# Attention units on TensorE regrouped by array tiling, the next tile's mask among the whole-array products

## The chip, the cores and the metric

The program runs on one core of one Trainium2 chip. The metric is device time in microseconds of one launch. The kernel before took 776.3 us (median of 3 runs, 775.83 to 776.98).

## The reference, cut to what matters

The program is an attention block and two mixture-of-experts layers one after the other. The attention (4 batches, 8 heads, 576 positions, head width 64) adds two parts: a softmax over keys pooled by four, and a local softmax over the keys less than four positions away.

```python
q_d = q.reshape(B, H, Sd, factor, D).mean(axis=3)      # k_d, v_d alike
out_up = np.repeat(sm_attn(q_d, k_d, v_d), factor, axis=2)
mask = np.abs(pos[:, None] - pos[None, :]) < factor     # factor = 4
scores = np.where(mask, scale * q @ k.T, -1e9)
out_local = softmax(scores) @ v
x = (out_up + out_local) rearranged to 2304 tokens x 512
x = moe(x)         # top-1 of 8 experts, tokens with x @ w_skip > 0
return moe2(x)     # top-2 of 8 experts, with noise on the logits
```

## The kernel before, in words

The first 130 us or so hold the attention, the rest the two expert layers. Attention is cut into **units**: 18 local tiles of 128 tokens (class `Local`, all 8 heads, four quarters of 32 tokens with a window of 38 keys each) and 5 pooled units per batch (class `Pooled`). `push(unit)` writes out one step of a software pipeline. TensorE, ScalarE and VectorE execute what `push` records in exactly that order; SyncE's queue of DMAs is ordered by the scheduler.

A step holds, for the newest unit, `scores` (products into a bank `pA`; for a local tile first a mask product with the whole array, L952, then 16 products of 32 columns, L958) and `soft` (VectorE: row maximum and difference, L965/L967 or L845/L848). For the unit two steps back it holds `turn` (transposes into `pT`, L983 or L859, and a ScalarE copy). Then come the step's fill functions, and among them or behind them the new unit's `exp` on ScalarE (L977 or L853), which waits for VectorE's `soft`. Last come the `values` of the unit three steps back (L996 for a local tile, L873 for a pooled unit) and VectorE's division (L1001, L877/L884).

The fill functions finish a token tile: `x_add` (adds the pooled part, L1007), `x_turn` (four transposes L1013, ScalarE copy L1015 into `xT`), in the next step `x_part` (products with the gate weights in four column strips of 32, L1022, ScalarE copy L1025 into `xpart`), and one step later `x_logits` (L1031, then L1032 on VectorE and L1033 on ScalarE) and the store of the tile (L1040 on SyncE's queue). `pool_v` (L805, L812) pools the values of a batch.

TensorE is used in two tilings. Whole-array products are those with 128x128 behind the operation's name in the trace (transposes, mask, logits, pooled scores and values). Column-tiled products address a strip of 32 columns and show as 128*32: the scores and values of local tiles, `x_part`, the fifth pooled unit of each batch and `pool_v`.

Buffers that matter here: `pT` has 3 banks, `pA` 2, `pB` 2; the copies `xT` have `NXT = 2` buffers; the finished tiles `x` have `XB = 8`. When no unit is left, `push(None)` drains the pipeline, and the last tiles pass through turn, part and logits behind each other; then TensorE turns the tokens gathered for the first expert (L541, `pT<-ident,xr`) and goes on with that expert's products (L562).

Of the kernel before, what the change touches and what calls it, by code (L numbers as in the profile page):

```python
# [23 lines left out]
NT = N // 128  # L24
# [3 lines left out]
W = 38  # L28
# [77 lines left out]
def moe_attention_kernel(ctx, tc, q, k, v, w_skip, w_gate, w1, w2, g2, n2, noise, u1, u2, out, dbg=None):  # L106
    nc = tc.nc
# [21 lines left out]
    def bank(tag, shape, dtype=F32):  # L129
        return psums[0].tile(shape, dtype, name=tag, tag=tag, bufs=psum_bufs[tag])  # L130
# [16 lines left out]
    identb = consts.tile([128, 128], BF, name="identb")  # L147
# [213 lines left out]
    late = rt.tile([128, NT], F32, name="late")  # L361
# [257 lines left out]
    with ExitStack() as actx:  # L619
# [92 lines left out]
        def mask(d):  # L712
            if d not in masks:
                distances(d)
                m = masks[d] = at.tile([128, 8, W], BF, name="mask" + "".join(map(str, d)), bufs=1)
                nc.vector.tensor_tensor(scr, dj[d], dj[d], op=OP.mult)
                nc.vector.tensor_scalar(m, scr[:, None, :].to_broadcast([128, 8, W]), 9.5, -8e9, op0=OP.is_gt,
                                        op1=OP.mult)
            return masks[d]

        offsets = [tuple(window(4 * t + s)[3] for s in range(4)) for t in range(NT)]
# [99 lines left out]
        class Pooled:  # L821
# [8 lines left out]
            def scores(self):  # L830
                b, u = self.b, self.u
                kd = kds[b % 2]
                assert held["kd", b % 2] == (b, 10)
                p = bank("pA", [128, 2, NPOOL])
                if u < 4:
                    nc.tensor.matmul(p, qd[b][:, u, 0:128], kd[:, u], start=True, stop=True)
                else:
                    for i in range(4):
                        nc.tensor.matmul(p[32 * i:32 * i + 32], qd[b][:, i, 112:144], kd[:, i], start=True,
                                         stop=True, tile_position=(0, 32 * i), skip_group_check=True)  # L840
                self.p = p
# [83 lines left out]
        def expand_up(t):  # L925

            b = B - 1
            p = ups[t] = bank(UPT, [128, DM])
            c = 64 + 128 * t - S * b
            x = expand[0]  # L930
            if t < NT - 1:
                nc.tensor.matmul(p, x[:, c:c + 128], od[b], start=True, stop=t > NT - 5, skip_group_check=True)
            for i in range(4):
                r, ci = p[:, i * 128:(i + 1) * 128], 64 + i * 128
                if t == NT - 5:
                    nc.tensor.matmul(r[0:64], x[:, ci + 64:ci + 128], ors[b - 1], start=False, stop=True,
                                     skip_group_check=True)
                elif t == NT - 1:
                    nc.tensor.matmul(r, x[:, ci:ci + 128], ors[b], start=True, stop=True, skip_group_check=True)

        class Local:
# [3 lines left out]
            def __init__(self, t):  # L945
                self.tile_no = t

            def scores(self):
                t = self.tile_no
                win = [window(4 * t + s) for s in range(4)]  # L950
                p = bank("pA", [128, 8, W])
                nc.tensor.matmul(p, identb, mask(offsets[t]), start=True, stop=False,  # L952
                                 skip_group_check=True)
                for i in range(4):
                    for s in range(4):
                        b, s0, ks, _ = win[s]
                        assert held["k", b % 2] == b
                        nc.tensor.matmul(p[s * 32:s * 32 + 32, 2 * i:2 * i + 2, :], qT[b][:, i, s0:s0 + 32],  # L958
                                         kTs[b % 2][:, :, i, ks:ks + W], start=False, stop=True,
                                         tile_position=(0, 32 * s), skip_group_check=True)  # L960
                self.p = p

            def soft(self):
                mx = at.tile([128, 8], F32, name="mx", bufs=NES)
# [78 lines left out]
        pipe = []  # L1043
        later = {}

        def schedule(n, f, *args):
            later.setdefault(len(pipe) + n, []).append(lambda: f(*args))

        drain = []
        wide = ep.tile([128, KF * CAPS[0]], F32, name="wide", tag="hT1")  # L1050
# [42 lines left out]

        def finish(t):
            if t in UPE:
                later.setdefault(len(pipe), []).insert(0, lambda: expand_up(t))
            elif t < SWIFT:
                schedule(UP, load_up, t)
            add = 0 if t in UPE else 2 if t >= SWIFT else ADD
            schedule(add, x_add, t)  # L1100
            add += STAY.get(t, 0)
            schedule(add + TURN, x_turn, t)
            schedule(add + PART, x_part, t)
            schedule(add + LOGIT, x_logits, t)
            if t == TA - 1:
                schedule(ADD + LOGIT - 4 + TA0, start_routing)

        def push(unit, *fill):
            fill = list(fill) + later.pop(len(pipe), [])
            pipe.append(unit)  # L1110
            if unit:
                unit.scores()
                unit.soft()
            if len(pipe) > D1 and pipe[-1 - D1]:
                pipe[-1 - D1].turn()
            for i, f in enumerate(fill):
                if i == 2 and unit:
                    unit.exp()
                f()
            if len(fill) <= 2 and unit:  # L1120
                unit.exp()
            if unit:
                for i in range(FILL + FILLS.get(len(pipe), 0)):
                    nc.tensor.matmul(wp, warm[:, 0:128], warm, start=True, stop=True)
            un = pipe[-1 - D2] if len(pipe) > D2 else None
            if un:
                un.values()
                t = un.tile_no
                if t is None:
                    if un.u == 3:  # L1130
                        ready.add(un.b)
                        if un.b == B - 1:
                            for n in range(SWIFT, UPE[0]):
                                schedule(0, load_up, n)
                else:
                    waiting.append(t)
                    if t + NVW < NT:
                        load_local(t + NVW)
            if started:
                run(early_1 or (early_2 if len(pipe) > PA else []), RS[min(len(started), len(RS)) - 1])  # L1140
                started.append(True)
                if len(pipe) > LA:
                    run(early_load, 1)
                if len(pipe) > LB:
                    run(early_load_2, 1)
                if len(pipe) > GA:
                    run(early_gather)
                if len(pipe) > TURN1:
                    run(early_turn)
                run(early_up, UP1.get(len(pipe), 0))  # L1150
            for i in range(1 if unit else DRAIN):
                if waiting and batch_of(waiting[0]) in ready:
                    finish(waiting.pop(0))
# [36 lines left out]
        pooled_after = {}  # L1190
# [3 lines left out]
        for t in range(NT):  # L1194
            for b in range(B):
                if LOADQK[b] == t:
                    load_qk(b)
                    if b in ONPOOLQD:
                        schedule(QDP, pool_q, b)
                if POOLQK[b] == t:  # L1200
                    for n in range(8):
                        schedule(n // QKS, pool_qk, b, n)
                    for n in range(3):
                        schedule(n // 2 if b in ONDVE else n, pool_qk, b, n + 8)
                if b == 0 and t == EXP4 and UPE:
                    schedule(0, expansion)
                if POOLV[b] == t:
                    schedule(0, pool_v, b, 0)
                    schedule(VS, pool_v, b, 1)
            if t == 3:  # L1210
                load_wall()
            if t < 3:
                schedule(0, lambda: None)
                schedule(0, lambda: None)
                schedule(0, (start_1, start_2, start_3)[t])
            push(Local(t))
            for b, u in pooled_after.get(t, []):
                push(Pooled(b, u))
        drain.append(True)
        while later or waiting or any(pipe[-D2:]):  # L1220
            push(None)
# [410 lines left out]
    with ExitStack() as mctx:  # L1632
# [20 lines left out]
        with none1.Else():  # L1653
            run(over1.steps[8:] + spilled())
            with tc.For_i(0, n_over1, 1) as i:
# [13 lines left out]
                p = bank("pH", [BLK1, 5, 1])  # L1669
# [34 lines left out]
        for e in range(E):  # L1704
# [9 lines left out]
            for f2 in range(KF // 2):  # L1714
# [6 lines left out]
                if f2 == 2 and e == 0:  # L1721
                    p = bank("pT", [BLK1, 3, C1])
# [57 lines left out]
    whole = Whole(weight_slot(F32), weight_slot(F32))  # L1780
# [78 lines left out]
    for e in range(1, E):  # L1859
# [17 lines left out]
        for b in range(NB2):  # L1877
# [6 lines left out]
            i = e * NB2 + b  # L1884
# [4 lines left out]
    with tc.If(n_over2 > 0):  # L1889
        with tc.For_i(0, n_over2, 1) as i:  # L1890
# [17 lines left out]
            p = bank("pH", [BLK2, 5, 1])  # L1908
# [10 lines left out]
            p = bank("pT", [128, KD, BLK2])  # L1919
# [6 lines left out]
            for f in range(KF):  # L1926
                p = bank("pH", [128, BLK2])
# [3 lines left out]
            p = bank("pY", [BLK2, DM])  # L1931
# [49 lines left out]
```

## Time and profile before

| | |
|---|---|
| median of 3 runs | 776.3 us |
| the profiled execution | 775.65 us |
| its span | 773.8 us |
| TensorE busy | 751.3 us, 97% |
| VectorE busy | 354.1 us, 46% |
| ScalarE busy | 249.1 us, 32% |
| granted TensorE clock, mean | 0.996 |

The span is the time between the first and the last profiled instruction. Busy shares are averages over stages with different limits: over the whole span VectorE is busy 46% of the time, but between 80 and 100 us 16.90 us of 20. TensorE's ends are modelled, so that "busy" there means occupied; the distance from one start to the next shows what a group of products really takes.

### The profile page before, as it was taken

The page shows a single profiled execution, that of the slowest core. Times are in us where ns is not written, and L with a number is a line of the kernel's source. Part 1 is how long each engine was busy: PE and PEld are TensorE (multiplying, and loading weights), DVE is VectorE, ACT ScalarE, POOL GpSimd, SP SyncE. Part 2 cuts the span into 40 slices and gives each one's busy share as a digit, 9 for nine tenths or more (in the row PEclk, how much of TensorE's full clock was granted, in tenths as well). Part 3 has the DMA queues.
Part 4 walks back from the last instruction along what each step waited for, and adds up shares of the span by engine and source line. Part 5 has one row for each costly group of instructions (what it writes and reads, how often), then busy time and mean ns, then how long its engine had stood idle before and what let it go on. Part 6 is the DMA issues. An engine that isn't in the chain of part 4 may idle for free.

```text
span 773.8 us, 15147 instructions
## 1 busy us (share of the span) xinstructions
PE 751.3 (97%) x6216; PEld 663.1 (86%) x6217; DVE 354.1 (46%) x794; ACT 249.1 (32%) x492; POOL 253.2 (33%) x259
## 2 busy tenths in 40 slices
PE   6799999999999999999999999999999999999996
PEld 3476777999999999988998998998997997987984
DVE  8886887411111755559864342352343342342200
ACT  3354553111112143224334333233333232333211
POOL 8781522220232432033565115115115125002012
PEclk9999999999999999999999999999999999999999
DMA  8898559599988872341647626426336336323013
GB/s 289 276 303 280 148 162 338 162 368 352 336 312 269 298 249 72 102 79 53 169 140 187 180 73 170 111 91 171 88 110 159 78 119 157 94 82 58 8 17 46
DMA packets 60264, 130.73 MB, mean 169 GB/s; under 512 B 15489, under 2 KB 16320, under 8 KB 58656
## 3 DMA queue, kind: packets, MB, share of 16 engines
q1 hardware_dynamic: 30688, 55.85, 22.9%
q0 software_dynamic: 12256, 27.21, 16.8%
q10 hardware_dynamic: 17248, 46.66, 16.7%
q8 instruction: 50, 0.82, 0.4%
q14 instruction: 22, 0.18, 0.1%
HBM read 101.86 MB, written 23.91 MB: 163 GB/s over the span
## 4 chain that ended last, share of the span: by engine, by line
PE 77%; issue 2%; DVE 1%; DMA 1%; POOL 0%; ACT 0%; POOLq 0%; DVEq 0%; ACTq 0%
PE pY L1622 27%; PE pH L1605 26%; PE pH L562 9%; PE pY L577 9%; PE pT L1590 2%; PE pT L599 1%; DMA rows<-x_d,ix2g 1%; PE pT L541 1%; PE pT L348 1%; PE pH L588 0%; POOL out L319 0%; DVE w L339 0%; PE pH L604 0%; PE pT L225 0%; DVE hl L1610 0%
## 5 line engine op out<-in xcount | busy, mean ns | idle before, releaser
L1622 PE MATMUL pY<-w,hh 128*128 128x512 f32 (+6 forms) x640 | 201.4, 396 | 0.0
L1605 PE MATMUL pH<-xh,w 128*128 128x256 f32 (+7 forms) x1024 | 195.9, 303 | 0.0
L1605 PEld LDWEIGHTS pH<-xh,w 128*128 128x128 f32 x1024 | 162.8, 188 | 0.8
L1622 PEld LDWEIGHTS pY<-w,hh 128*128 128x128 f32 (+6 forms) x640 | 115.0, 183 | 27.6
L1281 DVE TENSOR_TENSOR w<-stg,w 128x1024 fp32r<-128x1024 f32 x64 | 82.7, 1300 | 109.2 <-ACT w L1280 109.1
L1622 PE MATMUL pY<-w,hl 128*128 128x512 f32 (+6 forms) x320 | 125.7, 393 | 0.0
L1605 PE MATMUL pH<-xl,w 128*128 128x256 f32 (+7 forms) x512 | 123.4, 302 | 0.0
L1610 DVE SCALAR_TENSOR_TENSOR hl<-pH,hh 128x256 fp32r<-128x256 f32 (+7 forms) x128 | 56.9, 473 | 127.6 <-ACT hh L1609 127.3
L319 POOL DMA_INDIRECT out<-yo,ix2w x35 | 68.6, 1960 | 130.2 <-ACT yo L1624 121.6
L1609 ACT ACTIVATE hh<-pH 128x256 fp32r<-128x256 f32 (+7 forms) x128 | 49.2, 424 | 151.9 <-PE pH L1605 151.7
L1605 PEld LDWEIGHTS pH<-xl,w 128*128 128x128 f32 x512 | 90.2, 188 | 0.0
L314 POOL DMA_INDIRECT rows<-x_d,ix2g x32 | 36.2, 1130 | 155.0 <-PE pT L1590 144.2
L1622 PEld LDWEIGHTS pY<-w,hl 128*128 128x128 f32 (+6 forms) x320 | 58.5, 183 | 15.3
L1280 ACT ACTIVATE w<-stg 128x1024 fp32r<-128x1024 f32 x64 | 66.9, 1055 | 8.8 <-DMA stg<-in_moe_w 8.7
L577 PE MATMUL pY<-hT,w 128*128 128x112 f32 (+7 forms) x512 | 69.2, 296 | 0.0
L1624 ACT ACTIVATE yo<-pY,gt 128x512 f32<-128x512 f32 (+6 forms) x35 | 24.1, 688 | 138.2 <-PE pY L1622 77.3
L577 PEld LDWEIGHTS pY<-hT,w 128*128 128x128 f32 x512 | 67.4, 190 | 0.2
L562 PE MATMUL pH<-xT,w 128*128 128x200 f32 (+6 forms) x448 | 66.2, 301 | 0.0
L562 PEld LDWEIGHTS pH<-xT,w 128*128 128x128 f32 x448 | 61.1, 190 | 1.8 <-issue 1.7
L319 POOL DMA_INDIRECT l_d<-x,ix1w x15 | 14.3, 955 | 90.0 <-DVE x L607 89.1
L580 DVE COPY yT<-pY 128x224 f32<-128x224 f32 (+7 forms) x16 | 7.5, 471 | 73.9 <-PE pY L577 73.9
L1007 POOL TENSOR_TENSOR x<-x,up 128x512 f32<-128x512 f32 x15 | 19.5, 1306 | 41.3 <-DMA up<-od 30.4
(421 smaller groups left out, 858.6 us busy)
## 6 DMA issues: line engine op xcount, KB each, us to landing
w<-in_moe_w ACTq DMA_DIRECT2D x16, 2048.0 KB, 13.3
stg<-in_moe_w SPq DMA_DIRECT2D x64, 512.0 KB, 3.9
x_d<-x SPq DMA_DIRECT2D x18, 264.0 KB, 6.3
out<-zero ACTq DMA_DIRECT2D x3, 1536.0 KB, 8.5
qT<-in_q SPq DMA_DIRECT2D x3, 1152.0 KB, 5.8
vw<-in_v SPq DMA_DIRECT2D x18, 192.0 KB, 5.1
vw<-in_v ACTq DMA_DIRECT2D x18, 192.0 KB, 5.4
v<-in_v SPq DMA_DIRECT2D x3, 1024.0 KB, 9.2
```

The source lines that it names most:

```text
L314: return nc.gpsimd.indirect_dma_start(out=dst, out_offset=None, in_=x_d[0:n + 1], in_offset=bass.IndirectOffsetOnAxis(ap=idx, axis=0))
L319: return nc.gpsimd.indirect_dma_start(out=dst, out_offset=bass.IndirectOffsetOnAxis(ap=idx, axis=0), in_=src, in_offset=None, **kw)
L562: nc.tensor.matmul(self.p[:, j], w[:, k, f * 128:(f + 1) * 128], self.xT[:, k], start=k == 0, stop=k == KD - 1)
L577: nc.tensor.matmul(p[:, j], w[:, f, d * 128:(d + 1) * 128], self.hT[:, f], start=f == 0, stop=f == KF - 1)
L1007: e.tensor_tensor(xs[t][:, 0:DM], xs[t][:, 0:DM], ups[t], op=OP.add)
L1280: nc.scalar.activation(hi[:, c], st[i], AF.Copy)
L1281: V.tensor_tensor(lo[:, c], st[i], hi[:, c].bitcast(F32), op=OP.subtract)
L1605: nc.tensor.matmul(p, w[:, k, fs], self.x[ch][n][:, k, 0:ch[1] - ch[0]], start=k == 0 and i == 0, stop=k == KD - 1 and i == 2)
L1609: nc.scalar.activation(hi, p, AF.Relu)
L1610: V.scalar_tensor_tensor(lo, p, 0.0, hi.bitcast(F32), op0=OP.max, op1=OP.subtract)
L1622: nc.tensor.matmul(p, h[:, f], w[:, f], start=f == 0 and i == 0, stop=f == KF - 1 and i == 2)
L1624: nc.scalar.activation(o, p, AF.Copy, scale=gate[0:n])
```

## The change

Within a step the whole-array work now comes first and the column-tiled work last, a step's tiled products then lie next to the tiled scores of the next step's local tile. The mask product of a local tile leaves `scores` for a method `begin`, which is called one step earlier, ahead of the tiled work. `x_part` and `pool_v` are marked late and run behind the other fill functions, behind `exp`, behind the values of a pooled unit that uses the whole array, and behind the mask. Values that are column-tiled stay last.

```diff
+            def begin(self):
+                self.p = bank("pA", [128, 8, W])
+                nc.tensor.matmul(self.p, identb, mask(offsets[self.tile_no]), start=True, stop=False,
+                                 skip_group_check=True)
             def scores(self):
-                p = bank("pA", [128, 8, W])
-                nc.tensor.matmul(p, identb, mask(offsets[t]), start=True, stop=False,
-                                 skip_group_check=True)
         def schedule(n, f, *args):
-            later.setdefault(len(pipe) + n, []).append(lambda: f(*args))
+            late = (f in (x_part, pool_v))
+            later.setdefault(len(pipe) + n, []).append((late, lambda: f(*args)))
-        def push(unit, *fill):
-            fill = list(fill) + later.pop(len(pipe), [])
+        def push(unit, following=None):
+            fill = later.pop(len(pipe), [])
...
-            for i, f in enumerate(fill):
+            whole = [f for late, f in fill if not late]
+            for i, f in enumerate(whole):
                 if i == 2 and unit:
                     unit.exp()
                 f()
-            if len(fill) <= 2 and unit:
+            if len(whole) <= 2 and unit:
                 unit.exp()
...
             un = pipe[-1 - D2] if len(pipe) > D2 else None
+            early_values = un and un.tile_no is None and un.u < 4
+            if early_values:
+                un.values()
+            if isinstance(following, Local):
+                following.begin()
+            for late, f in fill:
+                if late:
+                    f()
             if un:
-                un.values()
+                if not early_values:
+                    un.values()
...
-            push(Local(t))
-            for b, u in pooled_after.get(t, []):
-                push(Pooled(b, u))
+            units = [Local(t) if t == 0 else upcoming] + [Pooled(b, u) for b, u in pooled_after.get(t, [])]
+            upcoming = Local(t + 1) if t + 1 < NT else None
+            if t == 0:
+                units[0].begin()
+            for unit, following in zip(units, units[1:] + [upcoming]):
+                push(unit, following)
```

TensorE, before: the step of the pooled unit whose scores start at 78.65 us, and the beginning of the next step, that of the local tile whose scores start at 81.60 us.

```order
L836 MATMUL pA<-kd_201,qd 128x288
L983 MATMUL pT<-ident,e_196 128x128 x4
L1022 MATMUL pT<-xT,wall 32x128 x4
L1013 MATMUL pT<-ident,x 128x128 x4
L873 MATMUL pB<-vd_243,epT 128x130
L873 MATMUL pB<-vd_243,epT 128x65 x2
L952 LDWEIGHTS identb
L952 MATMUL pA<-mask_179,identb 128x304
L958 MATMUL pA<-kT_240,qT 32x76 x16
L859 MATMUL pT<-ident,ep_253 128x128 x3
L1031 MATMUL pW<-sel,xpart 128x32
L1022 MATMUL pT<-xT,wall 32x128 x4
```

TensorE, with the change: the same place (line numbers behind the mask are one or two higher; the mask is L950).

```order
L836 MATMUL pA<-kd_201,qd 128x288
L984 MATMUL pT<-ident,e_196 128x128 x4
L1014 MATMUL pT<-ident,x 128x128 x4
L873 MATMUL pB<-vd_243,epT 128x130
L873 MATMUL pB<-vd_243,epT 128x65 x2
L950 LDWEIGHTS identb
L950 MATMUL pA<-mask_179,identb 128x304
L1023 MATMUL pT<-xT,wall 32x128 x4
L960 MATMUL pA<-kT_240,qT 32x76 x16
L859 MATMUL pT<-ident,ep_253 128x128 x3
L1032 MATMUL pW<-sel,xpart 128x32
```

The `x_part` products moved from between the two groups of transposes to the place just ahead of the next tile's scores; the order of everything else is kept. Counted over the attention, TensorE changes its tiling 122 times before and 86 times with the change.

ScalarE, before: the copies of the same step (`eT`, `xpart`, `xT`), its `exp` (`ep2`), and the first two of the next step.

```order
L986 ACTIVATE eT_1395<-pT_1390 128x512
L1025 ACTIVATE xpart_1402<-pT_1397 128x128
L1015 ACTIVATE xT_1409<-pT_1404 128x512
L853 ACTIVATE ep2_289<-ep2_289 128x2x144
L861 ACTIVATE epT_1452<-pT_1448 128x384
L1033 ACTIVATE x_759<-pW_1454 128x16
```

ScalarE, with the change: the same place.

```order
L987 ACTIVATE eT_1395<-pT_1390 128x512
L1016 ACTIVATE xT_1402<-pT_1397 128x512
L853 ACTIVATE ep2_289<-ep2_289 128x2x144
L1026 ACTIVATE xpart_1427<-pT_1422 128x128
L861 ACTIVATE epT_1452<-pT_1448 128x384
L1034 ACTIVATE x_759<-pW_1454 128x16
```

The copy `xpart` moved behind the step's `exp`. VectorE's order and GpSimd's are the same in both.

TensorE, before: the drain, from behind the turn of the tile `x_1874` (start 124.11 us) to the gathered tokens of the first expert.

```order
L1022 MATMUL pT_2217<-xT_2181,wall_83 32x128 x4
L1013 MATMUL pT_2224<-ident_77,x_2170 128x128 x4
L1022 MATMUL pT_2232<-xT_2215,wall_83 32x128 x4
L1013 MATMUL pT_2240<-ident_77,x_2073 128x128 x4
L1031 MATMUL pB_2248<-sel_85,xpart_2222 128x32
L1022 MATMUL pT_2253<-xT_2229,wall_83 32x128 x4
L1013 MATMUL pT_2260<-ident_77,x_2203 128x128 x4
L1031 MATMUL pB_2267<-sel_85,xpart_2237 128x32
L1022 MATMUL pT_2272<-xT_2245,wall_83 32x128 x4
L1031 MATMUL pB_2279<-sel_85,xpart_2258 128x32
L1022 MATMUL pT_2284<-xT_2265,wall_83 32x128 x4
L541 MATMUL pT_2294<-ident_77,xr0_160 128x112 x4
```

TensorE, with the change: the same place, behind the turn of that tile (now `x_1876`).

```order
L1014 MATMUL pT_2217<-ident_77,x_2170 128x128 x4
L1023 MATMUL pT_2225<-xT_2181,wall_83 32x128 x4
L1014 MATMUL pT_2233<-ident_77,x_2073 128x128 x4
L1032 MATMUL pB_2241<-sel_85,xpart_2230 128x32
L1014 MATMUL pT_2246<-ident_77,x_2203 128x128 x4
L1023 MATMUL pT_2253<-xT_2215,wall_83 32x128 x4
L1023 MATMUL pT_2260<-xT_2222,wall_83 32x128 x4
L1032 MATMUL pB_2267<-sel_85,xpart_2258 128x32
L1032 MATMUL pB_2272<-sel_85,xpart_2265 128x32
L1023 MATMUL pT_2277<-xT_2238,wall_83 32x128 x4
L1023 MATMUL pT_2284<-xT_2251,wall_83 32x128 x4
L541 MATMUL pT_2294<-ident_77,xr0_160 128x112 x4
```

A tile's part no longer stands ahead of the next tile's turn but behind it, and two tiles' parts stand side by side.

## Rows read from the trace of the kernel before

**Rows 1.** The page: the chain that ended last, shares of the span by engine.

```profile
PE 77%; issue 2%; DVE 1%; DMA 1%; POOL 0%; ACT 0%; POOLq 0%; DVEq 0%; ACTq 0%
```

**Rows 2.** One stretch of 20 us: length, busy time of each engine, PEclk, DMA share, GB/s.

```profile
80.00:100.00 20.00, 19.43 (x348) 15.38 (x341) 16.90 (x47) 10.60 (x30) 10.15 (x10) 1.00 0.60 156
```

**Rows 3.** Timeline, TensorE: start us, length us, engine, line, operation, out<-in, shape, count.

```profile
45.24 0.60 PE L983 MATMUL pT<-ident,e 128*128 128x128 f32 x4
45.67 0.78 PE L873 MATMUL pB<-vd,epT 128*128 128x130 f32 x6
...
82.65 0.31 PE L1031 MATMUL pW<-sel,xpart 128*128 128x32 f32 x2
82.89 0.42 PE L1022 MATMUL pT<-xT,wall 128*32 128x128 f32 x8
83.25 0.66 PE L1013 MATMUL pT<-ident,x 128*128 128x128 f32 x4
83.83 1.08 PE L996 MATMUL pB<-vw,eT 128*32 128x128 f32 x32
...
90.31 0.66 PE L1013 MATMUL pT<-ident,x 128*128 128x128 f32 x4
90.80 0.78 PE L873 MATMUL pB<-vd,epT 128*128 128x130 f32 x6
...
92.63 0.43 PE L1022 MATMUL pT<-xT,wall 128*32 128x128 f32 x8
92.87 1.06 PE L996 MATMUL pB<-vw,eT 128*32 128x128 f32 x32
```

**Rows 4.** Timeline, VectorE; in brackets the idle time ahead and what ended it.

```profile
72.28 0.69 DVE L1001 TENSOR_TENSOR x<-pB,sums 128x512 f32<-128x512 f32 x1 [2.53 <-DMA x_d<-x]
...
86.66 0.69 DVE L1001 TENSOR_TENSOR x<-pB,sums 128x512 f32<-128x512 f32 x1 [0.20 <-PE pW L1031]
...
88.71 0.17 DVE L877 RECIPROCAL rp<-pB 128x2 f32<-128x2 f32 x1 [0.38 <-PE pB L873]
...
115.83 0.69 DVE L1001 TENSOR_TENSOR x<-pB,sums 128x512 f32<-128x512 f32 x1 [0.24 <-PE pB L996]
```

**Rows 5.** Timeline, DMA issues of SyncE's queue.

```profile
51.15 0.56 SPq L644 DMA_DIRECT2D v<-in_v  x1
...
60.88 0.33 SPq L759 DMA_DIRECT2D qT<-in_q  x1
...
63.17 3.14 SPq L1040 DMA_DIRECT2D x_d<-x  x2
```

**Rows 6.** Timeline, ScalarE, the same two steps as the first order piece.

```profile
81.26 0.27 ACT L1025 ACTIVATE xpart<-pT 128x128 f32<-128x128 f32 x1
...
84.40 0.44 ACT L853 ACTIVATE ep<-ep 128x288 f32<-128x288 f32 x1 [2.38 <-DVE ep L848]
84.75 0.47 ACT L861 ACTIVATE epT<-pT 128x384 f32<-128x384 f32 x1
```

**Rows 7.** Timeline, TensorE, the drain.

```profile
124.11 0.60 PE L1013 MATMUL pT<-ident,x 128*128 128x128 f32 x4
...
128.45 0.42 PE L1022 MATMUL pT<-xT,wall 128*32 128x128 f32 x8
129.15 0.57 PE L541 MATMUL pT<-ident,xr 112*128 112x112 f32 x4 [0.28 <-DMA xr<-x_d,ix0g]
...
130.36 2.04 PE L562 MATMUL pA<-wide,w 128*128 128x112 f32 x16 [0.25 <-ACT wide L542]
```

**Rows 8.** Timeline, ScalarE, the drain.

```profile
124.74 0.60 ACT L1015 ACTIVATE xT<-pT 128x512 f32<-128x512 f32 x1 [1.94 <-PE pT L1013]
125.24 0.27 ACT L1025 ACTIVATE xpart<-pT 128x128 f32<-128x128 f32 x1
...
129.00 0.28 ACT L1025 ACTIVATE xpart<-pT 128x128 f32<-128x128 f32 x1
129.76 0.54 ACT L542 ACTIVATE wide<-pT 128x448 f32<-128x448 f32 x1 [0.49 <-PE pT L541]
```

More of the change, by code (lines that the diff above doesn't have):

```diff
@@ L946, in __init__ @@
                 self.tile_no = t
+            def begin(self):
+                self.p = bank("pA", [128, 8, W])
+                nc.tensor.matmul(self.p, identb, mask(offsets[self.tile_no]), start=True, stop=False,
+                                 skip_group_check=True)
             def scores(self):
-                t = self.tile_no
+                t, p = self.tile_no, self.p
                 win = [window(4 * t + s) for s in range(4)]
-                p = bank("pA", [128, 8, W])
-                nc.tensor.matmul(p, identb, mask(offsets[t]), start=True, stop=False,
-                                 skip_group_check=True)
                 for i in range(4):
@@ L960, in scores @@
                                          tile_position=(0, 32 * s), skip_group_check=True)
-                self.p = p
             def soft(self):
@@ L1095, in finish @@
             if t in UPE:
-                later.setdefault(len(pipe), []).insert(0, lambda: expand_up(t))
+                later.setdefault(len(pipe), []).insert(0, (False, lambda: expand_up(t)))
             elif t < SWIFT:
```

## The prediction

> **What bounds the kernel now.** I read the page's chain first: followed back from the end it covers the last 81% of the span, the two expert layers, and 77 of these 81 are TensorE [rows 1]. The expert layers are limited by TensorE, and they end earlier or later as the attention does. The question is what limits the attention. The stretches say that there TensorE is not alone: between 80 and 100 us VectorE is busy 16.90 us of 20 [rows 2]. So I went through VectorE's timeline for the places where it waits. From 72.28 us, when a transfer lets it go on after 2.53 us of idling, it works almost without a break; its waits for TensorE of over 0.3 us up to 115.83 are few, the first of them 0.38 at 88.71, and the last here is 0.24 [rows 4]. There VectorE starts the division after which come the indices of the first expert's tokens; they are gathered, and TensorE waits 0.28 us for them at 129.15 [rows 7]. Time that TensorE saves counts only if it passes these places. Then I read the drain, 124 to 130 us, instruction by instruction on TensorE and ScalarE [rows 7, 8], since nothing lies between it and the first expert.
>
> **What a change of tiling costs.** By starts in [rows 3]: the part products take 0.36 us up to a whole-array product (82.89 to 83.25) and 0.24 up to a tiled one (92.63 to 92.87), so leaving the tiling costs 0.12. Four transposes take 0.58 up to a tiled product (83.25 to 83.83) and 0.49 up to a whole one (90.31 to 90.80): going in costs 0.09. The same four take 0.43 when a whole product stands ahead too (45.24 to 45.67): another 0.06 just behind a tiled group. A pair of changes is worth some 0.25 us (0.12 + 0.09, and 0.06 in most places). The orders show 36 changes fewer, 18 pairs: 4.5 us if nothing else waited. Two pairs lie in the drain, five between 95 and 114 us, four between 78 and 88, seven ahead of 72.28.
>
> The Trainium skill ("TensorEngine Tiling (Array Packing)", Tiling Modes) states that a change of tiling mode, not just of the tile, drains TensorE; it gives no price. The trace agrees: 0.12 and 0.09 us. By that rule alone the change is worth the whole 4.5 us, the first rival below.
>
> **Term 1, up to 72.28 us.** VectorE stands there until the first tile's store has landed, because its buffer of `x` is needed again. The store was issued at 63.17, behind the loads of the next q and k from 60.88, which follow a load of v issued at 51.15 [rows 5]. Only what TensorE gains ahead of the load of v can move this chain: two mask pairs, 0.5 us. The other five pairs run into ScalarE, which here waits for the same transfers. Against it, the store can be issued later, since the tile's `xpart` copy now stands behind an `exp`. Bounds: -1.75 (seven pairs) and +0.5. I take -0.4, nearest to the two pairs.
>
> **Term 2, 72 to 116 us.** The copy `xpart` used to run at 81.26, ahead of an `exp` that waits 2.38 us for VectorE until 84.40 [rows 6]. In the new order it stands behind that `exp`. ScalarE works in order, so it starts at 84.75, where now the next copy starts, and ends at 85.02 (0.27 long). The logits product that needs it, at 82.65 now [rows 3], starts at 85.08: TensorE stands for 2.4 us. Behind the stalled product are the turn (0.44), the mask (0.23), the part (0.13 with the change into the tiling) and the values, which start at some 86.0 and not 83.83. They last 1.06 [rows 3], so VectorE's division starts at 87.1 or 87.2 and not 86.66 [rows 4]: +0.5. Most of the stall is covered because VectorE lags that far behind; the mask, too, now waits for VectorE one step earlier. Later the five pairs (1.25 us) win this back: two smaller stalls of the same kind, 0.3 us each, are in it. But beyond winning it back they bring little, since VectorE has almost no idle time left to give. Bounds: the 0.38 and 0.24 that VectorE waits in [rows 4], with about as much at the places between, give -1.2; if nothing is won back, with one more such stall, +1.0. I take 0: VectorE passes 115.83 on its old beat, shifted by term 1.
>
> **Term 3, the drain.** I call the tiles by their turns: P (`x_2119`), Q (124.11), R, S, T. `xT` has two buffers, so a copy for a turn waits until the part products two tiles back have read theirs. Before, each part stands ahead of the next turn and nobody waits. After, the order is turn Q, turn R, part P, turn S, logits P, turn T, part Q, part R, logits Q, logits R, part S, part T, gathered tokens. I use: turn 0.44 (0.53 ahead of a tiled product), part to its copy 0.55 (128.45 to 129.00), `xT` 0.60, the next ScalarE copy 0.50 after it (124.74 to 125.24), `xpart` 0.28, 0.06 for the hand-over [rows 3, 7, 8].
> - Turn R 124.55, part P 125.08. Copy R needs part P read: 125.63 to 126.23. P's `xpart` stands behind it: 126.13 to 126.41. Logits P 126.47, where TensorE has been free since 125.9.
> - Turn T 126.53, part Q 127.06. Copy S waits for part Q: 127.61 to 128.21. Part R takes the bank of S's transposes, so it starts at 128.27, 1.0 us late.
> - Copy T waits for part R: 128.82 to 129.42. The `xpart` copies of Q and R stand behind it, from 129.32, the second ending at about 129.76. Logits R 129.82.
> - Part S 130.06, part T 130.30, gathered tokens 130.66, against 129.15: +1.5. The copy `wide` follows after the same 0.61 and the first expert starts at 131.87 against 130.36 [rows 7, 8].
>
> So the two pairs saved in the drain turn into three waits on ScalarE, and the gather's 0.28 is covered. Bounds: 0, where the gather lands later than I think and sets the time in both orders, and +2.0, each wait a little longer. I take +1.5. Behind this place the order is the same and TensorE has no slack: it reaches the end.
>
> **The sum.** -0.4 + 0 + 1.5 = +1.1 us. On the profiled execution that is 775.65 + 1.1 = 776.75; its time lies 0.65 below the median of the three runs, so against the median 776.3 + 1.1 = 777.4 us.
>
> **The rivals.**
> 1. *The saved changes count in full*: the sixteen pairs ahead of the drain, 4.0 us, reach the gather. For it: TensorE is occupied 19.43 us of 20 [rows 2], which looks like the engine that bounds. Against it: VectorE at 16.90 of 20, whose work is not shortened, and the transfer at 72.28. With the drain's +1.5: 776.3 - 4.0 + 1.5 = 773.8.
> 2. *The copies behind `exp` cost more* (slower). Place: the logits products between 60 and 115 us, which wait for an `xpart` behind an `exp` behind VectorE. Price: 0.5 us at 86.66 and another 0.5 at 63 for the first store, not won back, and the drain in full: 776.3 + 0.5 + 0.5 + 1.5 = 778.8. It decides once VectorE has no idle time between 88.71 and 115.83 in which TensorE's five pairs can catch up.
> 3. *Nothing reaches the end*: VectorE and transfers hold the attention, and the gather lands so late that the drain's waits are under it: 776.3 with at most 0.3 more, 776.6. For it: TensorE already waits for the gather [rows 7]; against it, by 0.28 only.
>
> **How the numbers follow.** 0.2% is 1.55 us, about what a measurement of this kernel can tell from no change: 774.75 to 777.85. The forecast has a chance of 0.55; its own range is 776.3 to 778.6 (term 1 and 2 each 0.6 either way, the drain 0.4), of which 0.42 lies within 0.2% and 0.13 above. Rival 1 has 0.14, all faster; rival 2 has 0.21, all slower; rival 3 has 0.10, all the same. So faster 0.14, the same 0.52, slower 0.34. The range for 8 of 10 leaves out most of rival 1 and the far end of rival 2: 774.6 to 779.3.
>
> **What would show it.** Right: changes of tiling near 0.25 us a pair gone from TensorE; an idle time of some 2 us ahead of the logits product near 85 us, ended by ScalarE's `xpart`; VectorE's division near 72 us again ended by the store, at most half a microsecond earlier; in the drain three idle times on TensorE of 0.5 to 1 us, ended by `xpart` and `xT`, and no wait for the gather; from L541 to the end the same length as before. Wrong: the gather's index ready 2 us or more earlier than at 120 us (rival 1 holds), or the drain without those idle times, then my reading of the two `xT` buffers fails and the time falls below 776.

## The result, and the profile after

The changed kernel takes 782.2 us (median of 13 executions, 779.4 to 786.2); the kernel before took 776.3 beside it (774.7 to 778.1). The ratio is 1.0075 with a 95% interval of 1.0061 to 1.0088: 5.9 us slower (4.7 to 6.8). The forecast was 777.4 with 774.6 to 779.3: the sign is right, the size is not, and the range misses the median by 2.9 us.

The profiled execution took 782.92 us, its span is 781.1. The chain that ended last still names TensorE first (compare [rows 1]):

```profile
PE 75%; issue 2%; DVE 2%; DMA 1%; POOL 0%; ACT 0%; POOLq 0%; DVEq 0%; ACTq 0%
```

The busy time by stretch says more (length, busy time of TensorE, its weight loads, VectorE, ScalarE and GpSimd, then PEclk, DMA share, GB/s). The first line answers to [rows 2]:

```profile
80.00:100.00 20.00, 17.50 (x342) 14.45 (x341) 15.72 (x46) 10.37 (x29) 10.24 (x9) 1.00 0.59 153
...
127.00:132.40 5.40, 3.35 (x51) 2.25 (x46) 0.94 (x5) 2.56 (x8) 0.00 (x0) 1.00 1.04 369
132.40:139.20 6.80, 6.80 (x51) 6.36 (x43) 3.60 (x27) 2.20 (x8) 0.00 (x0) 0.50 0.81 248
```

TensorE is busy for 1.93 us less of the 20, since it stands more. In the drain it stands 2 of 5.4 us, and in the 6.8 us behind that its granted clock is 0.50, the lower of its two levels (1.2 GHz in place of 2.4). Before, there was no such stretch there.

TensorE's timeline of the drain, where [rows 7] showed one wait of 0.28 us for the gather:

```profile
128.10 0.41 PE L1032 MATMUL pB<-sel,xpart 128*128 128x32 f32 x2 [0.33 <-ACT xpart L1026]
128.35 0.64 PE L1014 MATMUL pT<-ident,x 128*128 128x128 f32 x4
...
130.11 0.42 PE L1023 MATMUL pT<-xT,wall 128*32 128x128 f32 x8 [0.78 <-ACT xT L1016]
131.48 0.63 PE L1032 MATMUL pB<-sel,xpart 128*128 128x32 f32 x4 [0.94 <-ACT xpart L1026]
132.04 0.80 PE L1023 MATMUL pT<-xT,wall 128*32 128x128 f32 x16
132.78 1.01 PE L541 MATMUL pT<-ident,xr 112*128 112x112 f32 x4
```

These are the three waits of the forecast: two for an `xpart` and one for an `xT`, and none for the gather. ScalarE's timeline shows why each copy into `xT` is late: its wait is ended by the part products that read the same buffer two tiles earlier (compare [rows 8]):

```profile
127.28 0.60 ACT L1016 ACTIVATE xT<-pT 128x512 f32<-128x512 f32 x1 [0.28 <-PE pT L1023]
127.78 0.27 ACT L1026 ACTIVATE xpart<-pT 128x128 f32<-128x128 f32 x1
129.46 0.60 ACT L1016 ACTIVATE xT<-pT 128x512 f32<-128x512 f32 x1 [1.41 <-PE pT L1023]
...
130.66 0.60 ACT L1016 ACTIVATE xT<-pT 128x512 f32<-128x512 f32 x1 [0.53 <-PE pT L1023]
131.16 0.44 ACT L1026 ACTIVATE xpart<-pT 128x128 f32<-128x128 f32 x2
```

In the units, the place of [rows 6] on ScalarE: the copy stands behind the `exp` that waits 2.23 us for VectorE.

```profile
85.62 0.45 ACT L853 ACTIVATE ep<-ep 128x288 f32<-128x288 f32 x1 [2.23 <-DVE ep L848]
85.97 0.26 ACT L1026 ACTIVATE xpart<-pT 128x128 f32<-128x128 f32 x1
```

TensorE's part product there, and the logits product that then waits for that copy:

```profile
83.21 0.29 PE L950 MATMUL pA<-mask,identb 128*128 128x304 bf16 x1
83.43 0.43 PE L1023 MATMUL pT<-xT,wall 128*32 128x128 f32 x8
83.67 0.71 PE L960 MATMUL pA<-kT,qT 128*32 128x76 f32 x32
...
86.28 0.41 PE L1032 MATMUL pW<-sel,xpart 128*128 128x32 f32 x2 [1.42 <-ACT xpart L1026]
```

The part now takes 0.24 us up to a tiled product (83.43 to 83.67): the 0.12 for leaving the tiling is saved, as [rows 3] had it. VectorE's divisions at the three places of [rows 4]:

```profile
73.50 0.69 DVE L1002 TENSOR_TENSOR x<-pB,sums 128x512 f32<-128x512 f32 x1 [2.96 <-DMA x_d<-x]
...
88.64 0.69 DVE L1002 TENSOR_TENSOR x<-pB,sums 128x512 f32<-128x512 f32 x1 [0.97 <-PE pB L997]
...
117.49 0.69 DVE L1002 TENSOR_TENSOR x<-pB,sums 128x512 f32<-128x512 f32 x1 [0.23 <-PE pB L997]
```

From these places the 7.3 us between the spans of the two profiled executions (781.1 and 773.8) can be split. The last column is a second profile of the changed kernel (run e5 below, 781.85 us with a span of 780.0), against the same profile of before:

| stretch | forecast | first profile | second profile |
|---|---|---|---|
| up to the division that waits for the store (72.28 before) | -0.4 | +1.22 | -0.35 |
| from there to the 15th division (43.55 before) | 0 | +0.44 | +2.04 |
| 15th division to L541 (13.32 before) | +1.5 | +1.97 | +1.82 |
| L541 to the first L577 (9.65 before) | 0 | +2.34 | +1.30 |
| behind that | 0 | +1.30 | +1.30 |

In what follows, the stretch from the division that waits for the store to the 15th division is called the middle.

### The profile page after: what moved, and what is told of

It is laid out like the page before. It is cut to its first block, busy times and chain, and to the rows that moved or that the text cites. A ratio compares the mean times of both kernels' runs of the same rounds, so it can differ in the third digit from the quotient of the medians.

```text
span 781.1 us, 15149 instructions
## 1 busy us (share of the span) xinstructions
PE 753.8 (97%) x6217; PEld 667.8 (85%) x6217; DVE 350.0 (45%) x794; ACT 249.4 (32%) x492; POOL 254.2 (33%) x259
## 4 chain that ended last, share of the span: by engine, by line
PE 75%; issue 2%; DVE 2%; DMA 1%; POOL 0%; ACT 0%; POOLq 0%; DVEq 0%; ACTq 0%
PE pY L1637 27%; PE pH L1620 26%; PE pH L562 8%; PE pY L577 8%; PE pT L1605 2%; PE pT L599 1%; DMA rows<-x_d,ix2g 1%; PE pT L348 1%; PE pT L541 1%; PE pT L225 0%; PE pH L588 0%; POOL out L319 0%; DVE na0lhs L339 0%; DVE na1lhs L339 0%; DVE w L339 0%
## 5 line engine op out<-in xcount | busy, mean ns | idle before, releaser
L577 PE MATMUL pY<-hT,w 128*128 128x112 f32 (+7 forms) x512 | 69.2, 296 | 0.0
L577 PEld LDWEIGHTS pY<-hT,w 128*128 128x128 f32 x512 | 67.5, 191 | 0.7 <-issue 0.5
L562 PE MATMUL pH<-xT,w 128*128 128x200 f32 (+6 forms) x448 | 66.2, 301 | 0.0
L562 PEld LDWEIGHTS pH<-xT,w 128*128 128x128 f32 x448 | 61.2, 191 | 1.8 <-issue 1.7
```

The costliest lines, as they stand in the source:

```text
L562: nc.tensor.matmul(self.p[:, j], w[:, k, f * 128:(f + 1) * 128], self.xT[:, k], start=k == 0, stop=k == KD - 1)
L577: nc.tensor.matmul(p[:, j], w[:, f, d * 128:(d + 1) * 128], self.hT[:, f], start=f == 0, stop=f == KF - 1)
```

## The experiments

Each ratio is to the kernel before, timed beside it on the same chip. A difference in microseconds is worked out from this ratio and is not always that of two medians.

**The drain.** Run e1 takes the drain back to the old order:

```diff
-            whole = [f for late, f in fill if not late]
+            whole = [f for late, f in fill if not late or not unit]
...
-                if late:
+                if late and unit:
```

> The changed kernel, but once no unit is left (the drain, from the last tiles to the first expert) the logits and part products stand in their old places. Theory: the change costs some 6 us, of which the drain's waits on ScalarE are 2.0 and the half clock that follows them 2.35; both go. 782.2 - 2.0 - 2.35 = 777.9 us, the granted clock full through the first expert, and the remaining +1.6 against the kernel before comes from ahead of 72 us. Rival, the half clock does not follow the drain's waits but comes anyway: 782.2 - 2.0 = 780.2. Rival, the drain's waits are covered by the gather: 782 and no change.

Measured: 778.2 us, ratio 1.0023 (1.0001 to 1.0046): +1.8 us (0.1 to 3.6). In its profile L541 comes 4.64 us behind the last division (6.94 in the changed kernel), and the clock is full behind it. So most of the loss is the drain. The clock was at its lower level in the units of this profile too, from 85.66 us for 3.41 us, behind a logits product that had waited 2.06 us for its `xpart`.

Run e2 is the opposite: the order of before in all units, and only the drain new (the selection of late functions applies to steps without a unit alone).

> The kernel before in all units (mask within the scores, parts and logits in their old places), only the drain in the new order. Theory: the drain alone costs its waits, 2.0 us, and the half clock behind them, 2.35: 776.3 + 4.3 = 780.6 us, with L541 some 2.0 us later behind the last mask than before, and the granted clock at its lower level for some microseconds from L541 on. Rival, no half clock: 778.3. Rival, the drain costs nothing by itself: 776.3.

Measured: 781.3 us, ratio 1.0078 (1.0054 to 1.0102): +6.0 us (4.2 to 7.9). The drain by itself makes a loss as large as the whole change. With the +1.8 of e1, which has the rest of the change, that is more than 5.9; both intervals are wide enough for the two to add up to it. Its profile has the same 0.78 and 0.94 us waits, and behind them

```profile
130.77:137.60 6.83, 6.83 (x43) 6.68 (x42) 4.32 (x33) 1.57 (x6) 0.00 (x0) 0.50 0.76 226
```

half the clock for 6.83 us. Run e3 keeps the order and gives `xT` a third buffer, for whose space `xpart` loses one:

```diff
-NXT = 2
+NXT = 3
...
-            c = at.tile([128, 128], F32, name="xpart", bufs=3)
+            c = at.tile([128, 128], F32, name="xpart", bufs=2)
```

> The changed kernel with three xT buffers in place of two (and two xpart buffers in place of three, for the space). Theory: the drain's waits come from two xT buffers: the copies for a turn no longer wait for the part two tiles back, so L541 comes 1 to 1.5 us earlier behind the last turns, a wait of 0.3 to 0.9 us ahead of a logits product is left, and the half clock goes or shrinks: 777.9 to 779. Rival, the waits are for ScalarE's own length of work and not for the buffers: drain as in the changed kernel, 782. Rival, two xpart buffers make new waits: above 782.

Measured: 777.05 us, ratio 1.0029 (1.0009 to 1.0049): +2.2 us. Of the waits, one is left on TensorE, L541 comes 5.20 us behind the last division, and no lower clock follows:

```profile
127.57 0.63 PE L1032 MATMUL pB<-sel,xpart 128*128 128x32 f32 x4 [0.73 <-ACT xpart L1026]
128.13 0.64 PE L1023 MATMUL pT<-xT,wall 128*32 128x128 f32 x16
```

The two `xT` buffers are thus the cause of two of the three waits and of most of the delay, as forecast; a wait for `xpart` is left without them. Run e4 leaves ScalarE's order and only keeps TensorE occupied in the waits, with eight products whose result nobody uses:

```diff
-BUSY = {}
+BUSY = {"part16": 3, "logits13": 4, "logits15": 1}
```

> The changed kernel with eight idle products added in the drain (whole array, result unused): three ahead of a part, four and one ahead of two logits products, where TensorE stands and waits for ScalarE. Theory: the half clock from 132.4 to 139.2 us follows those idle times; TensorE being busy in them keeps the full clock, which gives back 2.35 us and costs at most 0.3: 780.0. Rival, the clock does not depend on these idle times: 782.2 to 782.5, half clock in the same place.

Measured: 780.5 us, ratio 1.0070 (1.0047 to 1.0093). By time alone this doesn't tell the theories apart, its interval holds the changed kernel's ratio. The profile, taken of the fastest of the six executions (778.2), does:

```profile
126.82 0.82 PE L636 MATMUL pA<-warm 128*128 128x512 bf16 x3
127.66 0.43 PE L1023 MATMUL pT<-xT,wall 128*32 128x128 f32 x8
128.02 1.04 PE L636 MATMUL pA<-warm 128*128 128x512 bf16 x4
129.03 0.63 PE L1032 MATMUL pB<-sel,xpart 128*128 128x32 f32 x4
...
130.17 0.60 PE L541 MATMUL pT<-ident,xr 112*128 112x112 f32 x4
...
131.41 2.04 PE L562 MATMUL pA<-wide,w 128*128 128x112 f32 x16 [0.25 <-ACT wide L542]
```

Seven of the eight products are in these lines. Of the eighth the trace has only the weight load, at 125.05 ahead of the shortest wait. L541 is as late as ever behind the last division (6.79 us), but the 16 products of L562 take 2.04 us as in [rows 7], and the clock behind them is full. The 0.25 left at L562 is that of before. So in this profile the lower clock goes with TensorE's standing still, and not with the order of the work. What it costs in the median execution, this run doesn't show.

**The changed kernel again.**

> The changed kernel itself once more, for a second profile of it and for its time beside the three below on one chip. Theory: it is again some 5.9 us slower than the kernel before (781.6 to 782.2). Its second profile tells which parts of the first repeat: the drain's waits (+2.0 us to L541) and the half clock behind them must, the half clock near 43 us need not, and the time from the store that VectorE waits for near 72 us to the gathered tokens' division is 0.4 to 2 us longer than before. Rival: the early half clock is part of the change and comes at the same place again.

Measured: 782.9 us, ratio 1.0079 (1.0054 to 1.0104). The drain's waits repeat (0.78 and 0.95 us) and so does the lower clock, for 3.4 us this time. The same 16 products of L562 show what it costs there, 3.61 us and not 2.04:

```profile
133.90 3.61 PE L562 MATMUL pA<-wide,w 128*128 128x112 f32 x16 [0.25 <-ACT wide L542]
```

In the first profile the clock was at its lower level near 43 us as well (from 43.65 for 3.41 us); that doesn't repeat. Another is new, behind the logits' wait of 1.53 us at 84.72: half the clock from 86.02 to 89.43, in which the values take 1.83 us and not 1.08 [rows 3]:

```profile
84.72 0.41 PE L1032 MATMUL pW<-sel,xpart 128*128 128x32 f32 x2 [1.53 <-ACT xpart L1026]
...
85.90 1.83 PE L997 MATMUL pB<-vw,eT 128*32 128x128 f32 x32
```

The second profile's middle is 2.04 us longer than before, where the first, whose clock stayed full there, has 0.44.

**The units.** Run e6 moves the mask alone, with part and logits in their old places:

```diff
-            late = (f in (x_part, pool_v))
+            late = False
```

> Only the mask is moved, ahead of the values of the unit before; the part products stand in their old places, in the units and in the drain. That is 14 changes of tiling fewer, 7 pairs. Theory: no xpart copy stands behind exp, so the wait ahead of the logits product near 85 us is not there, and the saved pairs lie under VectorE and the store near 72 us: between -0.5 and +0.2 us, 775.8 to 776.5 where the kernel before has 776.3. Rival, the pairs count: 7 x 0.25 = 1.75 us less, 774.5. Rival, the early mask waits for VectorE and stops what is queued behind it: 777 or more.

Measured: 777.2 us, ratio 1.0016 (0.9992 to 1.0040). The interval holds no change as well as +3 us, so the time is inconclusive, though it excludes the 1.75 us of seven pairs. In the profile no logits product waits, and the middle lasts 43.59 us, as before (43.55).

Run e7 moves the parts alone, in the units only (the mask is put back into `scores`, the drain is that of e1):

> Only the part and pooled-value products are moved, and only in the units; the mask stands in the scores again, and the drain is the old one. That is 10 changes of tiling fewer. Theory: the xpart copy stands behind exp, the wait of about 2 us ahead of the logits product near 85 us is there, and the stretch between the division that waits for the store and the 15th one is 0.5 to 2 us longer than the 43.55 of before: 777 to 778.3. Rival, the mask is what costs: 776.3 or less.

Measured: 777.9 us, ratio 1.0023 (1.0002 to 1.0043). The wait is there, and half the clock with it:

```profile
81.16 0.64 PE L1033 MATMUL pW<-sel,xpart 128*128 128x32 f32 x2 [2.48 <-ACT xpart L1027]
```

```profile
80.42:87.24 6.82, 6.08 (x84) 4.77 (x85) 3.42 (x11) 2.30 (x7) 1.65 (x2) 0.50 0.21 69
```

In this profile the middle takes 47.05 us. With the mask in its old place the stall is there, and with the mask alone moved (e6) it isn't: not the mask but the copy behind `exp` costs. Run e8 tests that by moving `exp` behind the late functions, with everything else as in e1:

```diff
+            behind = unit and any(late for late, f in fill)
...
-                if i == 2 and unit:
+                if i == 2 and unit and not behind:
...
                 if late and unit:
                     f()
+            if behind:
+                unit.exp()
```

> The changed kernel with the old drain, and in the units the exp is issued behind the moved part products, so that their xpart copy stands ahead of it on ScalarE. All 32 saved changes of tiling of the units stay. Theory: with the old drain alone the kernel is 1.8 us slower than the one before, and this is the copy's wait behind exp; it goes, and 16 pairs of TensorE time with little to reach are left: between -1 and +0.3, 775.3 to 776.6. Rival, the loss is not this wait but the mask's place: 778, no change against the old drain alone. Rival, exp now waits for the part product and is late itself: above 778.

Measured: 775.3 us, ratio 0.9989 (0.9969 to 1.0008). I ran it a second time:

> The changed kernel with the old drain and with exp behind the moved part products, a second time, to tell its small gain from none. Theory: the five pairs of changes between the store that VectorE waits for and the 15th division count once the copy no longer stands behind exp; that stretch is 42.2 us again (43.55 before), and the time is 0.5 to 1.3 us below the kernel before on the same chip. Rival: the first result was chance and the time is that of before within 0.3 us.

Measured: 774.5 us, ratio 0.9987 (0.9969 to 1.0005). Both point to 0.9 to 1 us faster, and neither interval excludes no change. The mechanism is plain in the second one's profile, on ScalarE:

```profile
82.51 0.28 ACT L1026 ACTIVATE xpart<-pT 128x128 f32<-128x128 f32 x1
84.91 0.44 ACT L853 ACTIVATE ep<-ep 128x288 f32<-128x288 f32 x1 [2.13 <-DVE ep L848]
```

and on VectorE:

```profile
72.80 0.69 DVE L1002 TENSOR_TENSOR x<-pB,sums 128x512 f32<-128x512 f32 x1 [3.23 <-DMA x_d<-x]
...
87.17 0.69 DVE L1002 TENSOR_TENSOR x<-pB,sums 128x512 f32<-128x512 f32 x1 [0.20 <-POOL v L921]
...
114.98 0.69 DVE L1002 TENSOR_TENSOR x<-pB,sums 128x512 f32<-128x512 f32 x1 [0.24 <-PE pB L997]
```

The copy runs ahead of `exp`'s wait, the logits product doesn't wait, the division comes 14.37 us behind the store's (before 14.38), and the middle lasts 42.18 us, 42.22 in the first run of it. That is 1.37 and 1.33 us less than before.

**Ahead of 72 us.** A second profile of the kernel before, and nine idle products put into e8 near 43 us:

> The kernel before once more, for a second profile of it. Theory: the store that VectorE waits for near 72 us lands between 68 and 74 us from run to run, in the old order as in the new, and the stretch from there to the 15th division is again 43.5 to 43.6 us, with no half clock in it; the drain from the last division to the gathered tokens is again 4.6 to 5.0 us. Some 1.2 us that all profiles of changed kernels show behind 250 us against the first profile of before are in this second one too. Rival: those 1.2 us belong to the new orders and are not in it.

One execution, 777.46 us. VectorE's division behind the store starts at 74.20, the middle lasts 43.45, the drain 4.64 us:

```profile
74.20 0.69 DVE L1001 TENSOR_TENSOR x<-pB,sums 128x512 f32<-128x512 f32 x1 [2.11 <-DMA x_d<-x]
```

The division starts between 68.4 and 74.6 us in thirteen profiles, at 71.75, 72.28 and 74.20 with the old order ahead of it. The expected 1.2 us behind 250 us are not there; nor are they in e10 and e11, in the new order, so both the theory and its rival fall. From the first L577 to the end these three profiles take 0.30 to 0.51 us more than the first one of before, and the nine others, of which e6 and e2 have most of the old order, 1.15 to 1.99. So this time doesn't go with the order of the attention, as far as these runs show, and what it is they don't show.

```diff
                 else:
+                    for i in range(9 if b == 1 else 0):
+                        nc.tensor.matmul(wp, warm[:, 0:128], warm, start=True, stop=True)
```

> The same kernel as the one beside it, with nine idle whole-array products (result unused) ahead of the pooled scores near 43 us, where in two of four profiles of the new order TensorE stood 2.0 and 2.3 us for the pooled keys and the clock then fell to half for 3.4 us. Theory: with them there is no half clock at that place, and where the keys are early TensorE loses 2 us that the store near 72 us hides: 0.3 to 1 us below the kernel beside it. Rival, TensorE's time ahead of 72 us reaches the end after all: 1 to 2 us above it.

Measured: 774.7 us, ratio 0.9986 (0.9964 to 1.0008), beside 774.5 for e10 without them. By the medians neither the gain nor the loss came, though the spread of the two would hide a microsecond. The profile of e11:

```profile
44.35 1.89 PE L839 MATMUL pW<-warm 128*128 128x512 bf16 x8 [0.16 <-issue]
46.17 0.69 PE L841 MATMUL pA<-kd,qd 128*32 128x288 f32 x8
...
82.81 1.05 PE L1016 MATMUL pT<-ident,x 128*128 128x128 f32 x4 [1.90 <-POOL x L1010]
```

The added products occupy TensorE for 1.82 us (44.35 to 46.17), and the clock near 43 us stays full. That TensorE's time ahead of the store can't move the store is not shown: VectorE's division behind it starts at 74.57 here, the latest of the thirteen. This profile is also a third one of the order of e8. Its middle lasts 43.12 us, 0.43 less than before and not 1.3, and the clock fell in it, from 82.93 for 3.41 us, behind a wait of 1.90 us for GpSimd. In e10 the same transposes waited 1.46 us at 80.68, and the clock stayed full. Taking the copies out from behind `exp` thus removes one of the waits behind which the clock falls, but not all of them.

## Why the prediction was wrong, point by point

**The step that failed** is the end of term 3: "Behind this place the order is the same and TensorE has no slack: it reaches the end", and with it the sign of being right that went with it, "from L541 to the end the same length as before". I priced each wait by its own length and took what follows from rows at the full clock. After TensorE had stood 0.33, 0.78 and 0.94 us the clock fell to 1.2 GHz, and L541 to the first L577 took 2.34 us longer in the first profile and 1.30 in the second. Kept occupied in the same places, it didn't fall (e4). No term and no rival of the forecast had this. The Trainium skill has a rule on such drops ("TensorE: Matmul & The Clock Gate", Why this matters for your kernels): idle gaps of TensorE between bursts of products, beyond a length that it gives, let its throughput fall. The trace agrees on the effect but not on the length, since each of the three waits is under 1 us and shorter than the page's; by its rule they would have cost nothing more, and the measurement decides.

**Term 3, the waits themselves**: right in place, number and cause, sized +1.5 where +1.97 and +1.82 were measured, within its bounds of 0 to +2.0. What was too small in its working is the price of a logits product: 0.06 us for the one of P (126.47 to 126.53) and 0.24 for those of Q and R (129.82 to 130.06), where 0.25 (128.10 to 128.35) and 0.56 (131.48 to 132.04) were measured, 0.5 in all. The profile of before that it went by had a long drain itself: there L541 comes 4.98 us behind the last division, and 4.63 to 4.65 in seven others with the old drain. Against these the waits cost 2.2 to 2.3.

**Term 2** was +0.5 at the stall and then won back, 0 in sum. The stall is there, ended by `xpart` at the place named; priced at 2.4 us, it lasted 1.42 and 1.53 in the two profiles of the changed kernel. Up to the division it cost 0.76 us in the first, where the clock stayed full, and 1.5 to 1.8 where it fell around the stall (from the store's division the first profile takes 15.14, e5 15.91, e1 15.99, e3 16.21, and before it was 14.38). The winning back was wrong, too. That TensorE's saved pairs can win back 1.25 us there is right, but not with the stall: with it gone the middle is 1.33 and 1.37 shorter (e8, e10) and 0.43 in e11, where the clock fell. With the stall, the stretch from 86.66 on was just 0.32 us shorter in the first profile (28.85 and 29.17), and other copies stand behind `exp` there as well: a logits product at 112.89 still waits 0.57 for one. The second rival had this mechanism, at 0.5 us a place.

**Term 1**, -0.4, can't be measured: VectorE's division behind the store has a spread of 6 us over the profiles, and of 2.5 over the three with the old order ahead of it. Its reasoning is not refuted. Near 40 us TensorE was 2.4 us ahead in the first profile (its values start at 39.79, and before at 42.20), and VectorE still waited 2.96 us for the store.

**The price of a change of tiling**, 0.25 us a pair, and the first rival: by the rule of the Trainium skill cited there ("TensorEngine Tiling (Array Packing)", Tiling Modes) each change of tiling drains the array, so that 36 drains were to be saved. The trace agrees with the saving on TensorE (0.24 us in place of 0.36 for the part, above). That it counts in full is wrong: of the 4.0 us for 16 pairs ahead of the drain, the middle became 1.3 us shorter in two profiles of three with the copies ahead of `exp`, and not at all with the copies behind it. That even this reaches the end is not shown, since neither e8 nor e10 is clear of no change.

**The sum as measured**: the drain's waits 1.8 to 2.0, the lower clock behind them 1.3 to 2.3, the middle 0.4 to 2.0. In the first profile these make 4.75 us and in the second 5.16, and 5.9 (4.7 to 6.8) was timed. Both profiles have 1.30 more behind the first L577, which the change isn't shown to cause (see e9); so some 0.7 to 1.2 us of the loss are left open. That the waits in the units cost part of the time by the clock too is seen in e1, e3, e5 and e7, each of which has the lower clock around the stalled logits product or just behind it; in the first profile and in e4 (waits of 1.42 and 1.07 us) the clock didn't fall there. That filling this stall would keep the clock was not tried.

## What to carry to other kernels

Before products are grouped by tiling, look at what follows each group on the next engine in order: here a copy that slipped behind an instruction which waits for a third engine cost more than the changes of tiling saved. Price a wait of TensorE twice, once by its length and once for the products behind it, which may run at half the clock. And where few buffers stand between two steps, the order at the end of a pipeline, where no other work covers it, should be planned by itself; here the units could take the new order without a loss, with `exp` behind the copies, and the drain had to keep the old one. Even so no gain clear of the noise came of it.

## What the runs showed of the hardware

Three waits of 0.33, 0.78 and 0.94 us in the drain were followed by 3.4 to 6.8 us at half the clock, in three profiles of three with this drain unfilled, and in neither of the two where they were filled (e4) or one wait of 0.73 was left (e3). A single longer wait was followed by the lower clock in some profiles and not in others: 1.53 us in e5 and 1.42 in the first profile, at the same logits product. The busy share doesn't show it: over the 6.80 us at the lower clock TensorE is busy for 6.80 us.

Identical code differs by 2 us or more between executions for reasons ahead of it: the pooled scores near 43 us waited 2.25 us for GpSimd in the first profile, and not at all in e4 and e5, since GpSimd had started on the loads of `k` some 4 us later (at 28.57 there, where it waited 3.97 us for them, and at 24.54 and 24.51 in these).
